# Pooled attention and a GELU mixture layer on one core: the second attention's query casts move into the first MoE, and casts and transposing loads of the first attention are put in another order

## The chip, the core and the metric

The kernel runs on one core of a Trainium2 chip. A core has a matrix engine (TensorE, PE in the profile, with its weight loads as PEld), an engine for elementwise work and reductions (VectorE, DVE), one for functions such as exp and GELU (ScalarE, ACT), a general one (GpSimd, POOL) and SyncE (SP), which here only issues transfers. The engines run their own instruction streams in order and wait for one another through semaphores. Transfers (DMAs) issued by SP and by POOL are carried out by 16 DMA engines; the profile counts the two as queue q1 (SP) and queue q0 (POOL). The metric is device microseconds of one execution. Before the change the median of five runs is 951.9 us (957.32, 951.9, 951.82, 950.97, 953.35).

## The reference

Two stages follow one another: an attention of many queries on pooled keys, and a feed-forward layer with a sigmoid GELU. All inputs and outputs are float32 in memory.

```python
# q (4, 12288, 128), kv (4, 384, 32, 128), w_sr (128, 128)
kv_pool = kv.reshape(B, H // r, r, W // r, r, C).mean(axis=(2, 4))   # r = 4
kv_flat = kv_pool.reshape(B, -1, C) @ w_sr                           # 768 keys
k = v = kv_flat
s = scale * (q @ k.transpose(0, 2, 1))
s = s - s.max(-1, keepdims=True)
a = np.exp(s)
a /= a.sum(-1, keepdims=True) + 1e-09
attn = a @ v
# x = attn as (49152, 128), w_in (128, 2048), w_out (2048, 128)
h = x @ w_in
g = h * (1.0 / (1.0 + np.exp(-1.702 * h)))
out = g @ w_out
```

## The kernel before

**Tiling and stages.** The 49152 queries are cut into 96 groups of 512 (`G`, index i or g) and into 24 supertiles of 2048 (`SG`, index s, four groups each). A batch has 24 groups. The kernel goes through two rounds of 48 groups: first attention (groups 0 to 47), first MoE (the feed-forward layer for the same groups), second attention (48 to 95), second MoE. For one group the attention makes six score tiles, one for each 128 keys; the MoE makes sixteen hidden tiles of 128 features.

**The inner pattern.** `fill_attn` (L337) makes score matmuls into PSUM (L340) for three tiles at a time and ScalarE takes their exponential (L342); `fill_moe` (L583) does the same with L585 and the GELU (L587). `drain_attn` (L344) multiplies the exponentials with the values (L353), and VectorE normalizes the sums into x (L376, L379). `drain_moe` (L589) multiplies with w_out (L595); VectorE transposes the sum back (L606) into one of three buffers, and SP stores it (L608). PE makes fills and drains in turn.

**Who sets the order.** The instruction order of every engine is written out at build time. A loop at the end of the file plans it by a model of costs; `prepare` (L700) calls `background(i)` when the first tile of attention group i is filled, and `background_moe(g)` for an MoE group. These two issue all that the change touches, so "at group i" means this place in the order. The planner's costs do not depend on them.

**Queries.** Queries are needed in bfloat16 and transposed. The first three supertiles are loaded and transposed by PE. For the others `cast_q(s)` (L207, L209) has POOL issue a DMA that reads float32 queries and writes bfloat16 to a scratch tensor `q_bf`, 1 MB read and 512 KB written; later `load_qT(s)` (L212, L215) has SP issue a transposing load from there into one of four buffers qT, after a small memset by VectorE (L214). The load waits for its cast and for the last matmul that read the buffer. `TURN` and `CAST` (L513, L514) say at which group of the first attention each is issued; in the second attention `background` issues load i//4 + 3 and cast i//4 + 5 at every fourth group. Casts 13 to 16 are made in the first MoE at groups 19 to 22.

**Gates.** Before such a DMA `gate` (L506) has VectorE set one element and POOL overwrite it, so that POOL does not issue it before VectorE has come to that place.

**Scores for VectorE.** Some score tiles are not given to ScalarE: for the groups in `rolling` (38, 44, 57, 63, 69, 75, 81, 87) the last of the six, and all six of groups 48 to 51 (`early`), which are made during the first MoE. `early_fill` (L393) has PE compute such a tile (L405) in the midst of other work, and VectorE makes the exponential by a polynomial (L421 on). `early_fits` (L475) lets a rolling tile (i, 5) be made as soon as the groups in work are within one supertile of it: tile 5 of group 38 once group 32 has begun, from query load 9.

**x and its way to the MoE.** x is written by VectorE with queries on partitions, and the MoE needs features there. `put_away(n, m)` (L489, L493) has SP store a part of 24 tiles (six groups) to a scratch tensor `x_bf`, and `bring_back(n, m)` (L496, L499) has SP load it transposed into the same place. In the first attention this is done for parts 0 to 2, at groups 30 to 41, for the rest in the first MoE; in the second attention as the parts are finished. SP's queue is one: query loads, these transfers and output stores are issued in the order of the program.

**Other transfers on POOL.** `load_chunk(1, jc)` at groups 10 and 12 (keys of batch 1), the weights w_in (L540) and w_out (L543), and in the first MoE `add_kv` (L168, L173), eight steps for each of batches 2 and 3, at MoE groups 2 to 9 and 24 to 31.

Of the kernel before, what the change touches and what calls it, by code (L numbers as in the profile page):

```python
# [24 lines left out]
def kernel(  # L25
# [15 lines left out]
    NS = NG // 4  # L41
# [84 lines left out]
    def load_chunk(b, jc):  # L126

        a, ch = divmod(jc, HC)
        t = x_tile(XS - 1 - jc)
        nc.gpsimd.dma_start(out=t, in_=kv_r[b, a, ch])  # L130
        kv_tiles[b, jc] = t.rearrange("p (wp w1 c) -> p w1 wp c", w1=r, c=C)
# [36 lines left out]
    def add_kv(b, n):  # L168
        i, w = divmod(n, r)
        if n == 0:  # L170
            kv_sums[b] = kvsum.tile([Hp, 2, Wp, C], F32, name="kvs")
        for i2 in range(2):
            nc.gpsimd.dma_start(out=kv_sums[b][:, i2], in_=kv_p[b, i, w, :, i2],  # L173
                                **({"accum_op": ADD} if n else {}))
# [32 lines left out]
    def cast_q(s):  # L207
        sl = slice(s * SG, (s + 1) * SG)
        nc.gpsimd.dma_start(out=q_bf[sl, :].rearrange("(p i) c -> p (i c)", p=128),  # L209
                            in_=q_flat[sl, :].rearrange("(p i) c -> p (i c)", p=128))  # L210

    def load_qT(s):  # L212
        qTs[s] = qpool.tile([128, 1, SG], BF, name="qT")
        nc.vector.memset(qTs[s][:, 0, 0:1], 0.0)  # L214
        nc.sync.dma_start_transpose(out=qTs[s], in_=q_bf[s * SG:(s + 1) * SG, :])  # L215
# [273 lines left out]
    def put_away(n, m):  # L489
        size = PART // 2 if n == 0 and m > FIRST else PART  # L490
        for o in range(m * PART, m * PART + PART, size):
            lo = n * XS * SG + o * T
            nc.sync.dma_start(out=x_bf[lo:lo + size * T, :].rearrange("(k p) c -> p k c", p=T),  # L493
                              in_=x[:, o * T:(o + size) * T].rearrange("p (k c) -> p k c", k=size))

    def bring_back(n, m):  # L496
        o = m * PART
        lo = n * XS * SG + o * T
        nc.sync.dma_start_transpose(out=x[:, o * T:(o + PART) * T].unsqueeze(1), in_=x_bf[lo:lo + PART * T, :])  # L499
# [6 lines left out]
    def gate():  # L506

        one = gate_tile[:, gates[0] % 8:gates[0] % 8 + 1]
        gates[0] += 1
        nc.vector.memset(one, 0.0)  # L510
        nc.gpsimd.memset(one, 0.0)  # L511

    TURN = {6: 3, 7: 4, 8: 5, 19: 6, 21: 7, 24: 8, 27: 9, 29: 10, 32: 11, 36: 12}  # L513
    CAST = {0: 5, 13: 6, 14: 7, 19: 8, 22: 9, 25: 10, 28: 11, 32: 12}  # L514

    def background(i):

        first_round = i < GB * 2
        s = TURN.get(i, NS) if first_round else i // 4 + 3 if i % 4 == 0 else NS
        if s < NS:  # L520
            load_qT(s)
        s = CAST.get(i, NS) if first_round else i // 4 + 5 if i % 4 == 0 else NS
        if s < NS:
            gate()
            cast_q(s)
        if i in (10, 12):
            gate()
            for jc in range(i % 10 * 3 // 2, i % 10 * 3 // 2 + 3):
                load_chunk(1, jc)
        if 0 <= i - 16 < JC:  # L530
            extras.append((key_and_value, 1, i - 16))
        if 0 <= i - 15 < JC:
            extras.append((pool_chunk, 1, i - 15))
        if i in (30, 34, 38):
            put_away(0, (i - 30) // 4)
        if i in (33, 37, 41):
            bring_back(0, (i - 33) // 4)
        if i == 26:
            gate()
            nc.gpsimd.dma_start(out=w_in_sb, in_=moe_w_in)  # L540
        if i == 34:
            gate()
            nc.gpsimd.dma_start(out=w_out_sb, in_=moe_w_out.rearrange("(o p) c -> p o c", p=128))  # L543

    def background_moe(g):

        n, g = divmod(g, 4 * XS)
        m, odd = divmod(g - 9, 2)
        m += FIRST
        if n == 0 and FIRST <= m < RT // PART:  # L550
            (bring_back if odd else put_away)(n, m)
        g += n * 4 * XS
        nonlocal low
        if g == 12:
            low = EARLY * JC
            order[:] = [f for f in order if f >= low // K]
        if g == 40:
            background(early[0])
        if 19 <= g < 23:
            gate()  # L560
            cast_q(g - 6)
        if g in (34, 38):
            load_qT(13 + (g - 34) // 4)
        for b, lo in ((2, 2), (3, 24)):
            if lo <= g < lo + 8:
                gate()
                add_kv(b, g - lo)
            if g in (lo + 10, lo + 12):
                use_kv(b, (g - lo - 10) // 2)

    def use_kv(b, a):
        nonlocal extra_at
        sum_kv(b, a)
        on_dve(3.5)
        extra_at = max(extra_at, dve + 1.5)
        extras.extend([(transpose_pooled, b, a), (make_k, b, a), (make_v, b, a)])
# [123 lines left out]
    def prepare(p):  # L700

        nonlocal now
        kind, part = seq[p]
        for i, jc in part:
            if (kind, i) not in begun:
                begun.add((kind, i))
                (background if kind == "a" else background_moe)(i)
            while kind == "a" and ((key_and_value, i // GB, jc) in extras or (transpose_q, i) in extras):
                f, *args = extras.pop(0)
                now = max(now, free[next_acc()]) + COST[f][0]  # L710
                f(*args)
                free[last_acc] = copied(f)
# [73 lines left out]
    for n in range(len(seq)):  # L786
        fill(n + 2)
        jobs(n + 3)
        while True:
# [33 lines left out]
            kind, i, c = source[0]  # L823
# [58 lines left out]
```

## Time and profile before

| what | value |
|---|---|
| median of five runs | 951.9 us (950.97 to 957.32) |
| the profiled execution | 961.65 us |
| its span, first to last instruction | 959.9 us |
| granted TensorE clock, mean | 0.996 |
| ACT busy | 934.3 us |
| PE busy | 936.8 us |
| VectorE busy | 536.6 us |
| SP's queue q1: packets, bytes | 343872, 61.31 MB |
| POOL's queue q0: packets, bytes | 28656, 32.51 MB |
| query casts: number, median time to landing | 21, 6.7 us |
| query loads: number, median time to landing | 21, 7.3 us |
| transposing loads of x: number, median time to landing | 16, 7.6 us |

ACT's timeline gives the stages: the first attention's exponentials run to about 143 us, the first MoE's GELU from 143.8 to about 489, the second attention's from 489 to 615.6, the second MoE's from 616.9 to the end.

How to read it: durations and waits come from one profiled execution; the runs in the first row were made without the profiler. "Time to landing" counts from the issue of a transfer to its last byte's semaphore. A wait in the profile is an idle time of an engine and what ended it. Slices are fortieths of the span, a digit being tenths of busy time.

### The profile page before, as it was taken

Reading aid. Unit: us, or ns where it says so; the run is one execution under the profiler, and the core shown is the slowest. Engines: PE = TensorE matmul, PEld = TensorE weight load, DVE = VectorE, ACT = ScalarE, POOL = GpSimd, SP = SyncE. Lnnn points to the kernel's source line nnn. Section 1 sums busy time; section 2 is a strip of 40 time slices with the busy share of each in tenths; the row PEclk is TensorE's granted clock in tenths of the full one; section 3 lists DMA queues with packets and bytes.
Section 4 is the critical chain, followed back from the end, with each engine's and each line's share of the span. In section 5 each row is a group of like instructions: output and inputs, shape, how many; then the busy total and the mean of one; then the engine's idle time right before and its main releaser. Section 6 shows DMA issues by size and latency. Waiting matters only on the chain.

```text
span 959.9 us, 15315 instructions
## 1 busy us (share of the span) xinstructions
PE 936.8 (98%) x6201; PEld 503.6 (52%) x6314; DVE 536.6 (56%) x1039; ACT 934.3 (97%) x708; POOL 67.4 (7%) x117
## 2 busy tenths in 40 slices
PE   8999999999999999999999969999999999999998
PEld 3677776444444444444447747754444444444444
DVE  4643662111577776877755745365666665556631
ACT  5999999999999999999999959999999999999998
POOL 4100001320000341000000000000000000000000
PEclk9999999999999999999999989999999999999999
DMA  9999983999986898343258995462222222222222
GB/s 182 204 174 161 140 157 53 156 132 159 181 139 92 118 154 102 56 77 55 44 95 160 110 169 119 112 134 41 36 42 39 39 39 39 41 36 43 35 44 45
DMA packets 372871, 94.93 MB, mean 99 GB/s; under 512 B 346736, under 2 KB 370416, under 8 KB 372464
## 3 DMA queue, kind: packets, MB, share of 16 engines
q1 hardware_dynamic: 343872, 61.31, 39.6%
q0 software_dynamic: 28656, 32.51, 22.7%
q8 instruction: 49, 0.80, 0.4%
q14 instruction: 22, 0.18, 0.1%
q10 hardware_dynamic: 272, 0.13, 0.0%
HBM read 52.49 MB, written 48.76 MB: 105 GB/s over the span
## 4 chain that ended last, share of the span: by engine, by line
PE 55%; ACT 40%; DMA 4%; issue 1%; DVE 0%; POOL 0%; POOLq 0%
ACT ag L587 34%; PE banks L595 18%; PE banks L585 17%; PE banks L353 9%; PE banks L340 9%; ACT ag L342 6%; DMA qT<-q_bf 3%; DMA x<-in_kv_dram 1%; PE banks L405 1%; PE banks L139 0%; PE banks L623 0%; PE banks L233 0%; ACT L587 0%; PE banks L161 0%; DVE kT L163 0%
## 5 line engine op out<-in xcount | busy, mean ns | idle before, releaser
L587 ACT ACTIVATE ag<-banks 128x1536 bf16<-128x1536 f32 (+1 forms) x510 | 682.2, 1507 | 0.0
L585 PE MATMUL banks<-x,w_in_sb 128*128 128x512 bf16 x1485 | 407.5, 379 | 2.0 <-ACT ag L587 0.3
L595 PE MATMUL banks<-ag,w_out_sb 128*128 128x512 bf16 x1476 | 403.2, 379 | 1.9
L342 ACT ACTIVATE ag<-banks 128x1536 bf16<-128x1536 f32 (+2 forms) x192 | 246.1, 1424 | 14.0 <-PE banks L340 11.1
L595 PEld LDWEIGHTS <-w_out_sb 128*128 128x128 bf16 x1520 | 148.5, 98 | 178.0 <-issue 0.9
L585 PEld LDWEIGHTS <-w_in_sb 128*128 128x128 bf16 x1522 | 147.3, 98 | 170.4 <-issue 1.1
L606 DVE STREAM_TRANSPOSE o_sb<-banks 128x512 f32<-128x512 f32 x95 | 67.9, 715 | 211.1 <-PE banks L595 197.9
L353 PEld LDWEIGHTS <-ag 128*128 128x128 bf16 x2272 | 146.7, 98 | 47.3 <-issue 2.2
L353 PE MATMUL banks<-v,ag 128*128 128x129 bf16 x2272 | 164.7, 220 | 0.6 <-issue 0.4
L340 PE MATMUL banks<-qT,kT 128*128 128x512 bf16 x499 | 145.8, 380 | 3.5 <-DVE kT L163 1.0
L432 DVE SCALAR_TENSOR_TENSOR ea<-ea,eb 128x512 f32<-128x512 f32 x128 | 87.8, 686 | 3.4 <-issue 0.2
L376 DVE RECIPROCAL rec<-banks 128x3 f32<-128x3 f32 x124 | 22.3, 180 | 97.4 <-PE banks L353 97.2
L379 DVE TENSOR_TENSOR x<-banks,rec 128x384 bf16<-128x384 f32 x124 | 69.1, 557 | 4.3
L340 PEld LDWEIGHTS <-kT 128*128 128x128 bf16 x544 | 46.4, 98 | 26.6 <-DVE kT L163 1.7
L463 DVE RECIPROCAL eb<-ea 128x256 f32<-128x256 f32 x28 | 47.6, 1726 | 0.5
L421 DVE TENSOR_SCALAR ea<-banks 128x512 f32<-128x512 f32 x32 | 22.1, 692 | 41.4 <-PE banks L405 41.1
L173 POOL DMA_DIRECT2D kvs<-in_kv_dram x32 | 40.5, 1308 | 18.1 <-DMA kvs<-in_kv_dram 14.1
L456 DVE SCALAR_TENSOR_TENSOR ea<-ea,eb 128x512 f32<-128x512 f32 x56 | 38.3, 685 | 1.6
L511 POOL MEMSET gate_tile<- 1x1 f32 x39 | 4.1, 106 | 445.4 <-DVE gate_tile L510 445.4
L427 DVE SCALAR_TENSOR_TENSOR eb<-eb,ea 128x512 f32<-128x512 f32 x32 | 22.1, 690 | 0.9
L405 PE MATMUL banks<-qT,kT 128*128 128x512 bf16 x32 | 12.4, 386 | 8.5 <-DMA qT<-q_bf 8.5
L443 DVE TENSOR_SCALAR qT<-banks 128x512 f32<-128x512 f32 x14 | 9.7, 692 | 17.2 <-PE banks L399 16.9
(84 smaller groups left out, 271.1 us busy)
## 6 DMA issues: line engine op xcount, KB each, us to landing
out_dram<-o_sb SPq DMA_DIRECT2D x380, 64.0 KB, 2.0
kvs<-in_kv_dram POOLq DMA_DIRECT2D x32, 384.0 KB, 6.4
q_bf<-in_q_dram POOLq DMA_DIRECT2D x21, 512.0 KB, 6.7
x_bf<-x SPq DMA_DIRECT2D x12, 768.0 KB, 5.8
x<-in_kv_dram POOLq DMA_DIRECT2D x12, 512.0 KB, 10.9
x_bf<-x SPq DMA_DIRECT2D x8, 384.0 KB, 4.0
x<-in_q_dram POOLq DMA_DIRECT2D x5, 256.0 KB, 14.9
w_in_sb<-in_moe_w_in_dram POOLq DMA_DIRECT2D x1, 512.0 KB, 5.4
```

The costliest lines, as they stand in the source:

```text
L173: nc.gpsimd.dma_start(out=kv_sums[b][:, i2], in_=kv_p[b, i, w, :, i2], **({"accum_op": ADD} if n else {}))
L340: nc.tensor.matmul(ps[:, k, :], kTs[i // GB][:, jc * 128:(jc + 1) * 128], rhs, start=True, stop=True)
L342: nc.scalar.activation(place([("a",) + c for c in chunks]), ps, AF.Exp, scale=scale)
L353: nc.tensor.matmul(av_of[u][:, k * (C + 1):(k + 1) * (C + 1)], weights(("a", i, jc))[:, o:o + T], vs[i // GB][:, jc, 0:C + 1], start=(jc = ...
L379: nc.vector.tensor_tensor(to, ps[:, :, 0:C], rec.unsqueeze(2).broadcast_to([128, TS, C]), MUL)
L432: nc.vector.scalar_tensor_tensor(a, a, COEFFS[k], b, ADD, MUL)
L456: nc.vector.scalar_tensor_tensor(a, a, COEFFS[k], b, ADD, MUL)
L463: nc.vector.reciprocal(b[:, m:m + 256], a[:, m:m + 256])
L585: nc.tensor.matmul(ps[:, k, :], w_in_sb[:, fc * 128:(fc + 1) * 128], x[:, g % (4 * XS) * G:(g % (4 * XS) + 1) * G], start=True, stop=True)
L587: nc.scalar.activation(place([("m",) + c for c in chunks]), ps, AF.Gelu_apprx_sigmoid)
L595: nc.tensor.matmul(o_of[g], w_out_sb[:, fc, :], weights(("m", g, fc)), start=(fc == 0), stop=(fc == FCH - 1))
L606: nc.vector.transpose(o_sb, o_of.pop(g))
```

## The change

Casts 17 to 23, made during the second attention before, are made in the first MoE, at groups 33 to 39; casts 13 to 16 move one group later there, to 20 to 23 (`CAST_MOE`). The second attention makes no cast. Query loads 13, 14 and 15 move from MoE groups 34, 38 and 40 to 41, 42 and 43.

In the first attention cast 8 moves from group 19 to 15, casts 9 and 10 are issued together at 25 and casts 11 and 12 at 26. Query loads 6 to 12 are issued at groups 20, 21, 22, 30, 32, 35 and 40 (19, 21, 24, 27, 29, 32 and 36 before). The put-aways of x are issued at 28, 33 and 38 (30, 34, 38), its transposing loads at 31, 36 and 41 (33, 37, 41). The load of w_in moves from 26 to 27 and that of w_out from 34 to 28.

```diff
-    TURN = {6: 3, 7: 4, 8: 5, 19: 6, 21: 7, 24: 8, 27: 9, 29: 10, 32: 11, 36: 12}
-    CAST = {0: 5, 13: 6, 14: 7, 19: 8, 22: 9, 25: 10, 28: 11, 32: 12}
+    TURN = {6: 3, 7: 4, 8: 5, 20: 6, 21: 7, 22: 8, 30: 9, 32: 10, 35: 11, 40: 12}
+    CAST = {0: [5], 13: [6], 14: [7], 15: [8], 25: [9, 10], 26: [11, 12]}
+    CAST_MOE = {20: 13, 21: 14, 22: 15, 23: 16, 33: 17, 34: 18, 35: 19, 36: 20, 37: 21, 38: 22, 39: 23}
...
     def background(i):
...
-        s = CAST.get(i, NS) if first_round else i // 4 + 5 if i % 4 == 0 else NS
-        if s < NS:
+        if i in CAST:
             gate()
-            cast_q(s)
+            for s in CAST[i]:
+                cast_q(s)
...
-        if i in (30, 34, 38):
-            put_away(0, (i - 30) // 4)
-        if i in (33, 37, 41):
-            bring_back(0, (i - 33) // 4)
-        if i == 26:
+        if i in (28, 33, 38):
+            put_away(0, (i - 28) // 5)
+        if i in (31, 36, 41):
+            bring_back(0, (i - 31) // 5)
+        if i == 27:
             gate()
             nc.gpsimd.dma_start(out=w_in_sb, in_=moe_w_in)
-        if i == 34:
+        if i == 28:
             gate()
             nc.gpsimd.dma_start(out=w_out_sb, in_=moe_w_out.rearrange("(o p) c -> p o c", p=128))
...
     def background_moe(g):
...
-        if g == 40:
+        if g in CAST_MOE:
+            gate()
+            cast_q(CAST_MOE[g])
+        if g in (41, 42):
+            load_qT(g - 28)
+        if g == 43:
             background(early[0])
-        if 19 <= g < 23:
-            gate()
-            cast_q(g - 6)
-        if g in (34, 38):
-            load_qT(13 + (g - 34) // 4)
```

## The prediction

> **What bounds the kernel now.** I read the page first: the span, the busy times, the slices.
>
> ```profile
> span 959.9 us, 15315 instructions
> PE 936.8 (98%) x6201; PEld 503.6 (52%) x6314; DVE 536.6 (56%) x1039; ACT 934.3 (97%) x708; POOL 67.4 (7%) x117
> PE   8999999999999999999999969999999999999998
> ACT  5999999999999999999999959999999999999998
> ```
>
> ScalarE (ACT) computes for 934.3 of 959.9 us, and the change gives it no other work: the lists of exponentials and activations, and which of them VectorE makes, stay. The whole prize is ACT's idle time, 25.6 us. The slices put it at the start, at the end, and in one slice near 550 us. The waits and ACT's timeline name that one.
>
> ```profile
> ACT ag L342 <- PE banks L340: 11.1, 5, 9.9
> PE banks L405 <- DMA qT<-q_bf: 8.5, 1, 8.5
> ```
>
> ```profile
> 550.03 4.13 ACT L342 ACTIVATE ag<-banks 128x1536 bf16<-128x1536 f32 x3 [0.26 <-PE banks L340]
> 564.02 1.45 ACT L342 ACTIVATE ag<-banks 128x1536 bf16<-128x1536 f32 x1 [9.85 <-PE banks L340]
> 565.63 1.45 ACT L342 ACTIVATE ag<-banks 128x1536 bf16<-128x1536 f32 x1 [0.16 <-PE banks L340]
> ```
>
> In the second attention TensorE (PE) waited 8.5 us for a transposing load of queries, at a score matmul for VectorE (L405), and ACT behind it lost 9.85 us, 1.4 more than PE (8.47 in PE's timeline). With the two small gaps beside it the stall is 9.85 + 0.26 + 0.16 = 10.3 us. Why the load was late is in the timelines of the SP and POOL queues and in the time that single DMAs took to land.
>
> ```profile
> 528.16 6.61 SPq L499 DMA_TRANSPOSE x<-x_bf  x1
> 534.87 25.44 SPq L215 DMA_TRANSPOSE qT<-q_bf  x2
> ```
>
> ```profile
> 531.13 0.49 POOL L209 DMA_DIRECT2D q_bf<-in_q_dram  x1
> 541.82 0.49 POOL L209 DMA_DIRECT2D q_bf<-in_q_dram  x1
> ```
>
> ```profile
> x<-x_bf SPq DMA_TRANSPOSE x1, 20.3
> q_bf<-in_q_dram POOLq DMA_DIRECT2D x1, 512.0 KB, 19.1
> qT<-q_bf SPq DMA_TRANSPOSE x1, 26.2
> ```
>
> These three are the load of x issued at 528, the cast of 541.8 and the query load of 534.9. Once the casts are over, the same two kinds of load (571.2 and 577.1) take this:
>
> ```profile
> x<-x_bf SPq DMA_TRANSPOSE x1, 8.3
> qT<-q_bf SPq DMA_TRANSPOSE x1, 4.6
> ```
>
> So casts under transposing loads stretch 8.3 to 20.3 and 4.6 to 26.2 us. Now the sum that matters most. The profiled execution took 961.65 us, 1.75 around its span. Without the 10.3 us it would have taken **951.4**. The median of the runs shown is 951.9, the lowest 950.97: the stall is in the profiled execution, and perhaps in the run of 957.32, but hardly in the median one. The change can take 10 us from a profile and about 0.5 from the median.
>
> **The change, part by part.**
>
> *Second attention: seven casts (17 to 23) go.* What remains there is the regime of 567 us on. The load that stalled (issued 534.9, supertile 20 for group 81) would land after 4.6 to 9.1 us (the latter is the row at 519.7, with a cast beside it): 544 at the latest, against PE's stop at 552.65. Gain 10.3 us in the profiled execution; in the median run I take its excess over the floor, 0.5.
>
> *First MoE: those seven casts come to groups 33 to 39, casts 13 to 16 move from 19-22 to 20-23.* Each issues a gate (VectorE memset 59 ns, POOL memset 0.1 us) and one DMA on POOL's queue. The nearest rows are the casts of 279 to 300 us, already in this MoE, landing in 5.9 to 6.7 us while ACT is busy throughout. What hides them: casts have nothing behind them on POOL until the key/value sums begin at group 24 (315.3 us; cast 16, at about 307.5, lands near 314), and the last sum lands at 373.8, before group 33 (380.2). Output stores on SP have three buffers and one group (some 6.75 us) each, so a store a few us late costs nothing. Without that cover one cast would cost its 6 us. Gates: 19 before, 17 after. Zero.
>
> *Query loads 13, 14, 15 move from groups 34, 38, 40 to 41, 42, 43 of the MoE.* ACT's starts of those groups are 436.6, 444.7 and 451.4; the slowest load there took 7.4 us, so they land by 444, 452, 459. They are first read from 487 (13, and 14 by a matmul of L405) and 499 (15, the same way). Their buffers (loads 9, 10, 11) were last read in the first attention. The output stores queued behind them on SP wait for an issue of 1.6 to 5.3 us, inside the buffers' slack. Zero.
>
> *First attention: order on POOL and SP.* Cast 8 goes from group 19 to 15: it then queues behind cast 7 (landed 64.7) at the 2.44 us by which casts 6 and 7 landed one after the other, so it is down at 67.2. Query load 6 (group 20, about 66.3) thus meets almost no cast; at 4.0 to 9.2 us it lands at 70 to 75.5, and PE reads it at about 75.5 (ACT starts that group at 77.5, and PE's timeline fills some 2 us ahead of it). Loads 7 and 8 (69 and 71.6) have over 10 us. The put-aways and returns of x keep landing before the MoE (146.8 us). Weights w_in and w_out come at groups 27 and 28. All zero, but for one edge.
>
> **The edge is query load 9.** It moves from group 27 (issued 85.45) to 30. Its first reader isn't group 36 (ACT 110.0) but a score matmul for VectorE, chunk (38, 5), which the planner places once group 32 has begun:
>
> ```profile
> 100.69 0.38 PE L405 MATMUL banks<-qT,kT 128*128 128x512 bf16 x1
> ```
>
> VectorE's memset for a load stands at 90.96 for group 29 and 99.00 for 32, so load 9 is issued near 93.7 and has 7.0 us. What lies in its way: casts 9 and 10 issued at 79.2, 11 and 12 at 83.2, w_in at 85.3, w_out at 87.2, and on SP put-away 0 at 87.1 (5.7 to 6.4 us). The first cast lands 5.9 us after its issue (row of 79.4), 85.1, the next three at 2.44 each, 92.4; w_in moves as many bytes, 94.9; then w_out, of which no undisturbed row exists (18.9 us amid loads). The rows for a query load, issued at 91.1 (tail of a cast), 85.4 (w_in and a cast), 99.1 (a cast and a put-away):
>
> ```profile
> qT<-q_bf SPq DMA_TRANSPOSE x1, 7.0
> qT<-q_bf SPq DMA_TRANSPOSE x1, 9.5
> qT<-q_bf SPq DMA_TRANSPOSE x1, 12.4
> ```
>
> From 4.6 us (alone) to 12.4, load 9 lands at 98.3 to 106.1, and PE waits 0 to 5.4; with the 1.4 of the known stall ACT loses 0 to 6.8. By the row it is nearest to, 7.0, it lands at 100.7 and nothing is lost.
>
> Here the Trainium skill speaks against the change ("DMA: Bandwidth & Descriptors", section on issuing engines not being separate queues): DMAs from SP and POOL interleave on the same 16 engines, so taking turns in program order frees nothing while the bunch is unfinished. As an estimate by that rule: from 93.7 the engines still owe w_in's last 1.2 us, w_out at no less than 2.44, and the query load's own 4.6, 8.2 in all: landing 101.9, PE waits 1.2, ACT loses up to 2.6, a total of 954.0. By the row it is 951.4. The rows of 20 and 26 us show that sharing can be worse than the rule. I stay with the row, as the unprofiled median shows less of such waits than the profile, and add 0.1 for a rare miss: **951.5**.
>
> **Rivals.**
> 1. *The edge is missed a little* (load 9 takes 8 to 10.4 us): 1 to 4.8 us lost, 952.4 to 956.2; still no measurable change. For: the rule's sum. Against: w_out may be light.
> 2. *Slower: load 9 lands late, at L405 near 100.7.* At 12.4 us the loss is 6.8: **958.2**. It decides from a latency of 10.4 us (0.5% is 4.8 us, less 1.4, gives 3.4 of PE wait). For: w_out took 18.9 us amid loads, and the row of 99.1. Against: no cast is issued after 83.7 until the MoE.
> 3. *Faster:* the stall sits in every run, and an execution without it is quicker than the profile's floor. Time if the median loses 5 us: 946.9. Against: five runs from 950.97 would all have to hold it, beside a floor of 951.4.
> 4. *The change does nothing to the stall*, as the loads slow one another without casts: 951.9. Against: 8.3 and 4.6 from 567 us on.
>
> **How the numbers follow.** 0.5% (4.8 us) is about what a measurement of this kernel can tell from no change: below 947.1, above 956.7. Chances: forecast 0.48, rival 1 0.20, rival 4 0.08, rival 2 0.18, rival 3 0.06. The first three are within, 0.76. The range starts at 949.4, below which only rival 3 and a little luck lie (the stall-free span is 949.6), and ends at 958.2, where rival 2's row ends: about 0.08 is left above and 0.08 below.
>
> **What would show it.** Right: ACT without a gap between 485 and 615; no cast after 425; query loads of 4.6 to 6 and x loads near 8.3 in the second attention; a span near 949.6. At L405 near 100.7 no DMA wait, with load 9 down by then. Wrong: PE waiting there for qT, ACT idle behind it by 1.4 more; or output stores holding VectorE in MoE groups 33 to 43; or a profile without gaps whose runs are yet well under 949, which would mean that the unprofiled runs held stalls unseen.

## The result, and the profile after

Over 44 runs the changed kernel takes 950.99 us in the median (950.48 to 952.62). The kernel before, over 79 runs of the same measurement, takes 953.38 (950.47 to 967.6). The ratio of the means is 0.9962, with a 95% interval of 0.9949 to 0.9975: 0.38% faster (the medians alone differ by 0.25%). Two of the 79 runs, 966.87 and 967.6, over 1.5% above the fastest, are left out of the ratio. The time is inside the range of the prediction and the change, as it said, within 0.5%; but the interval excludes no change, and the gain lies where the prediction had put next to none, in the median run. The five runs shown before had a median of 951.9. The 79 have quartiles of 951.07 and 958.09, a mean of 955.04, and 30 of them are above 956.7. Of the 44 runs after, none is, and the mean is 951.14. So the change hardly moved the best run (950.47 before, 950.48 after). It removed the spread. As the experiments below show, that spread is the stall of the second attention, which cost most executions something, and more than 6 us in 30 of the 79.

The page of the changed kernel, the same rows as before:

```profile
span 949.2 us, 15311 instructions
PE 935.7 (99%) x6201; PEld 503.0 (53%) x6314; DVE 536.8 (57%) x1037; ACT 934.1 (98%) x708; POOL 66.9 (7%) x115
PE   8999999999999999999999999999999999999998
ACT  5999999999999999999999999999999999999998
```

ACT works as long as before (934.1 us against 934.3) and the span of this profiled execution is 10.7 us shorter: all but 0.2 of it is idle time that is gone. The 5 near 550 us is a 9. ACT's timeline across the second attention is now one piece of 86 activations between two table loads:

```profile
487.96 1.28 ACT L342 ACT_TABLE_LOAD   x1
489.26 115.71 ACT L342 ACTIVATE ag<-banks 128x1536 bf16<-128x1536 f32 x86
604.99 1.28 ACT L588 ACT_TABLE_LOAD   x1
```

SP's queue in the stretch of the stall (start, duration, what), and then the time to landing of the load of x at 528 and of the query load at 534:

```profile
528.26 6.03 SPq L499 DMA_TRANSPOSE x<-x_bf  x1
534.39 9.12 SPq L215 DMA_TRANSPOSE qT<-q_bf  x2
```

```profile
x<-x_bf SPq DMA_TRANSPOSE x1, 8.6
qT<-q_bf SPq DMA_TRANSPOSE x1, 5.7
```

They were 20.3 and 26.2 us with casts beside them. The edge that the prediction named is there too. The query load 9 is issued at 93.19, takes this long to land, and PE comes to its first reader at the same moment (PE's timeline; the bracket is the wait):

```profile
qT<-q_bf SPq DMA_TRANSPOSE x1, 7.5
100.78 0.39 PE L405 MATMUL banks<-qT,kT 128*128 128x512 bf16 x1 [0.18 <-DMA qT<-q_bf]
```

### The profile page after: what moved, and what is told of

Same layout as the page of the kernel before. It is cut to its first block, busy times and chain, and to the rows that moved or that the text cites. A ratio compares the mean times of both kernels' runs of the same rounds, so it can differ in the third digit from the quotient of the medians.

```text
span 949.2 us, 15311 instructions
## 1 busy us (share of the span) xinstructions
PE 935.7 (99%) x6201; PEld 503.0 (53%) x6314; DVE 536.8 (57%) x1037; ACT 934.1 (98%) x708; POOL 66.9 (7%) x115
## 4 chain that ended last, share of the span: by engine, by line
ACT 88%; PE 8%; DMA 3%; issue 1%; DVE 0%; POOLq 0%
ACT ag L588 71%; ACT ag L342 16%; PE banks L340 4%; PE banks L353 3%; DMA x<-in_kv_dram 2%; DMA qT<-q_bf 1%; PE banks L586 0%; PE banks L624 0%; PE banks L139 0%; ACT L588 0%; PE banks L596 0%; ACT L342 0%; PE banks L233 0%; PE banks L161 0%; DVE kT L163 0%
## 5 line engine op out<-in xcount | busy, mean ns | idle before, releaser
L340 PE MATMUL banks<-qT,kT 128*128 128x512 bf16 x499 | 145.0, 379 | 3.5 <-DVE kT L163 1.0
L173 POOL DMA_DIRECT2D kvs<-in_kv_dram x32 | 40.4, 1320 | 18.4 <-DMA kvs<-in_kv_dram 15.1
L434 DVE SCALAR_TENSOR_TENSOR ag<-ea,ee 128x512 bf16<-128x512 f32 x24 | 16.5, 688 | 0.7
```

Source lines behind the costliest of these rows:

```text
L340: nc.tensor.matmul(ps[:, k, :], kTs[i // GB][:, jc * 128:(jc + 1) * 128], rhs, start=True, stop=True)
```

## The experiments

Each was timed in turn with the kernel before, on one chip, in four series. "Before" below is its median there, 954.66, 955.06, 954.74 and 953.97 in the four series, with a lowest run of 950.29 to 950.36 each time.

### Which part of the change does it

The seven casts alone, everything else as before:

```diff
-        s = CAST.get(i, NS) if first_round else i // 4 + 5 if i % 4 == 0 else NS
+        s = CAST.get(i, NS) if first_round else NS
...
         if 19 <= g < 23:
             gate()
             cast_q(g - 6)
+        if 33 <= g < 40:
+            gate()
+            cast_q(g - 16)
```

> Before, with casts 17 to 23 alone moved to groups 33 to 39 of the first MoE; the first attention and all query loads stay. Theory (the stall comes from casts in flight beside transposing loads in the second attention): all of the gain, a median of 951.0 to 951.5 and a spread of some 2 us, no DMA wait in the profile's second attention. Rival (the first attention's order is part of the gain): a median above 952, runs up to 957 left.

Measured: 950.58 us (950.40 to 951.74, 14 runs), ratio to before 0.9955 (0.9935 to 0.9976), no DMA wait in its second attention. The casts are all of the gain; it is even 0.4 us under the whole change.

The rest of the change alone:

```diff
-    CAST_MOE = {20: 13, 21: 14, 22: 15, 23: 16, 33: 17, 34: 18, 35: 19, 36: 20, 37: 21, 38: 22, 39: 23}
+    CAST_MOE = {20: 13, 21: 14, 22: 15, 23: 16}
...
+        if not first_round and i % 4 == 0 and i // 4 + 5 < NS:
+            gate()
+            cast_q(i // 4 + 5)
```

> The changed kernel with casts 17 to 23 put back into the second attention, so only the new order of the first attention and the later query loads 13 to 15 are left. Theory: like before, median 952 to 955, runs up to 960 and more, a wait at L405 near 561 us in many executions. Rival (first attention's order pays): at most 952 with a narrow spread.

Measured: 956.19 us (950.76 to 962.61, 14 runs), ratio 1.0005 (0.9975 to 1.0034). The stall is back in its profile at the same place: PE's wait, and the query load behind it.

```profile
PE banks L405 <- DMA qT<-q_bf: 7.5, 1, 7.5
qT<-q_bf SPq DMA_TRANSPOSE x1, 25.6
```

The rest of the change, the new order of the first attention above all, gains nothing by itself that these runs show.

### Which casts

Only casts 22 and 23 back at groups 68 and 72, where x is put away and loaded:

```diff
+    CAST = {..., 25: [9, 10], 26: [11, 12], 68: [22], 72: [23]}
+    CAST_MOE = {..., 36: 20, 37: 21}
```

> The changed kernel with only casts 22 and 23 back in the second attention (groups 68 and 72), where x is put away and loaded transposed. Theory in its narrow form (a cast harms where it meets a transposing load of x): as bad as before, median 952 to 955, runs over 957. Rival (it is the number of casts in that stage): about two sevenths of it, median near 951.6, no run over 954.

Measured: 953.79 us (950.70 to 959.10, 22 runs), ratio 0.9994 (0.9974 to 1.0014); six runs over 956.7. Two of the seven casts bring the slowness back, as the narrow theory has it. Its profiled execution was one of those that escaped (span 949.1 us, no wait at L405 in this stage), but the loads in it are slow all the same, the one of x at 528.1 and the query load at 534.5. The query load landed at 548.9, and PE had stopped for it at 552.65 in the kernel before: a slow load costs nothing until it outlasts that slack.

```profile
x<-x_bf SPq DMA_TRANSPOSE x1, 16.2
qT<-q_bf SPq DMA_TRANSPOSE x1, 14.5
```

The other five back instead, casts 22 and 23 left in the MoE:

```diff
+    CAST = {..., 48: [17], 52: [18], 56: [19], 60: [20], 64: [21]}
+    CAST_MOE = {..., 38: 22, 39: 23}
```

> The changed kernel with casts 17 to 21 back in the second attention (issued at MoE group 43 and at groups 52 to 64), casts 22 and 23 left in the MoE. Narrow theory: no loss, median 951.0 to 951.5, no run over 953; query loads of some 9 us beside a cast, but none over 12. Rival (number of casts): five sevenths of it, median above 952, runs over 955.

Measured: 950.97 us (950.46 to 952.61, 18 runs). Five casts in the second attention cost nothing. The query load issued beside the cast of 509 us landed in 8.8, against 3.7 in the changed kernel without a cast: slower, but far within its slack. So not the number of casts counts, but their place: casts 22 and 23 run beside the loads of x, which begin at 528. What else is particular to that place (a put-away of x stands just before each of these loads) was not varied by itself.

### The edge at query load 9

```diff
-    TURN = {..., 30: 9, 32: 10, 35: 11, 40: 12}
+    TURN = {..., 31: 9, 32: 10, 35: 11, 40: 12}
```

> The changed kernel with query load 9 issued at group 31 in place of 30, some 2.7 us later. Theory (the matmul of L405 near 100.7 us is the first reader, and PE has nothing in hand there): load 9 lands at 102.5 to 103.5, PE waits 1.8 to 2.8 us, ACT loses that and up to 1.4 more, median 952.5 to 955. Rival (the load finds a freer queue when it is later, or PE and ACT make up for it): the same as the changed kernel, within 0.7 us of 951.0.

Measured: 951.15 us (950.58 to 951.99, 22 runs). The load came 1.4 us later, not 2.7 (94.63 against 93.19), and landed at 101.69. In the profile PE waited for it, and ACT lost about the same, not 1.4 more:

```profile
101.74 0.39 PE L405 MATMUL banks<-qT,kT 128*128 128x512 bf16 x1 [1.37 <-DMA qT<-q_bf]
102.98 8.16 ACT L342 ACTIVATE ag<-banks 128x1536 bf16<-128x1536 f32 x6 [1.44 <-PE banks L340]
```

The profiled execution took 951.99 us, the slowest of the 22; the median is that of the changed kernel. So the median is where the rival put it; the matmul of L405 is the first reader and PE does wait, as the theory has it, but too briefly to be seen in the median.

With `27: 9` in its place, so that the load meets the bunch of casts 9 to 12:

> The changed kernel with query load 9 issued at group 27, as before, so beside casts 9 to 12. Theory (in the changed kernel load 9 lands just as it is needed and costs at most 0.3 us): 950.7 to 951.2, that is no difference. Rival (casts under the load stretch it as in the second attention): a landing after 100.7, a wait at L405, 952 or more.

Measured: 952.43 us (951.85 to 954.98, 22 runs), 1.4 above the changed kernel's 950.99; here the rival was right. Issued 8.1 us earlier than in the changed kernel (85.05), the load landed later (102.44), PE waited 2.1 us, and ACT lost 2.14.

```profile
qT<-q_bf SPq DMA_TRANSPOSE x1, 17.4
PE banks L405 <- DMA qT<-q_bf: 2.1, 1, 2.1
```

So letting the casts go first is worth something once they are bunched. What is left of the edge is the end of that bunch, and so w_out was moved behind the query loads:

```diff
-        if i == 28:
+        if i == 41:
             gate()
             nc.gpsimd.dma_start(out=w_out_sb, in_=moe_w_out.rearrange("(o p) c -> p o c", p=128))
```

> The changed kernel with the load of w_out taken from group 28 to group 41, behind the query loads. Theory (what keeps load 9 back in the changed kernel is the end of POOL's bunch, w_out last, and that costs the 0.4 us by which it is above the run that moves the seven casts alone): load 9 lands at 97 to 98.5, no DMA wait at L405, median 950.5 to 950.7. Rival (the 0.4 us lies elsewhere in the first attention or is chance): 951.0 to 951.2, whatever load 9 does.

Measured: 950.50 us (950.30 to 950.69, 12 runs), ratio 0.9958 (0.9932 to 0.9985). Load 9 landed at 98.32, after the time below, and no PE wait for a query load is left.

```profile
qT<-q_bf SPq DMA_TRANSPOSE x1, 5.5
```

The changed kernel itself, put beside three other experiments as a control, gave this:

> The changed kernel itself, beside the others on one chip. 950.9 to 951.2; if it is that, the kernel before with casts of 1 KB (950.56) is 0.4 us faster than it.

Measured: 951.23 us (950.70 to 952.43, 12 runs).

The slowest of the 12 runs with w_out moved (950.69) is not above the fastest of these 12, though they are from another series. By these medians the edge cost the changed kernel 0.5 to 0.7 us, and the version with w_out moved is level with the best found.

### What in a cast does the harm

In the packet records a cast of the kernel before writes one packet of 32 KB on each of the 16 DMA engines; a transposing load consists of 256-byte packets. The cast's two rearrangements were cut into blocks, first in the kernel before:

```diff
-        nc.gpsimd.dma_start(out=q_bf[sl, :].rearrange("(p i) c -> p (i c)", p=128),
-                            in_=q_flat[sl, :].rearrange("(p i) c -> p (i c)", p=128))
+        nc.gpsimd.dma_start(out=q_bf[sl, :].rearrange("(h p i) c -> p h (i c)", p=128, h=4),
+                            in_=q_flat[sl, :].rearrange("(h p i) c -> p h (i c)", p=128, h=4))
```

> Before, with each cast cut into four row blocks, so that a partition's run of it is 2 KB of float32 instead of 8 KB; bytes, places and order stay. Theory of turns by packet (a small packet of a transposing load waits out a long packet of a cast): smaller cast packets shorten the loads, the wait near 561 us is under 4 us or gone, median 951 to 952. Rival (any cast in flight beside a transposing load of x does it, whatever its packets): like before, median 952 to 955, runs over 957.

Measured: 950.56 us (950.30 to 951.04, 20 runs), ratio 0.9945 (0.9928 to 0.9962). No cast was moved, and the stall is gone. First the page's count of POOL's packets in the kernel before, then in this one:

```profile
q0 software_dynamic: 28656, 32.51, 22.7%
```

```profile
q0 software_dynamic: 39072, 32.51, 23.3%
```

The bytes are the same; 10416 packets more over 21 casts are 496 for each, from 16 of 32 KB to 512 of 1 KB. The load of x, the cast and the query load that took 20.3, 17.0 and 26.2 us in the kernel before (issued at 528, 531 and 535) take here, in the same places:

```profile
x<-x_bf SPq DMA_TRANSPOSE x1, 10.8
q_bf<-in_q_dram POOLq DMA_DIRECT2D x1, 512.0 KB, 8.1
qT<-q_bf SPq DMA_TRANSPOSE x1, 8.3
```

The cut shortens the runs that a cast reads as well as those that it writes, so these runs do not tell the two apart.

With 8 KB packets in the kernel before (p=16, h=4 in the same rearrangement):

> Before, with each cast written in runs of 8 KB (four blocks over 16 partitions), between the 32 KB packets of before and the 1 KB of the run that lost the stall. Theory (a load waits out whole packets): between the two, the load of x issued near 528 lands in 11 to 16 us, a median of 950.6 to 952.5, few runs over 955. Rival (any split that makes more than one packet per DMA engine is enough): 950.5 to 950.7, as at 1 KB.

Measured: 951.01 us (950.38 to 955.53, 12 runs; mean 952.23). That lies between, five of 12 runs being over 952. The profiled execution had a stall, PE waiting 2.9 us; its load of x took 18.4 us, outside what was expected, and its query load 20.7.

```profile
x<-x_bf SPq DMA_TRANSPOSE x1, 18.4
qT<-q_bf SPq DMA_TRANSPOSE x1, 20.7
PE banks L405 <- DMA qT<-q_bf: 2.9, 1, 2.9
```

The same 1 KB casts in the changed kernel, and in the one with load 9 at group 27:

> The changed kernel with every cast written in runs of 1 KB (four row blocks), the form that removed the stall from the kernel before. Theory (packets of 32 KB were all that the casts did to the loads, and the changed kernel has nearly none left): 950.4 to 950.8, at most 0.6 us under the changed kernel. Rival (the bunch of four casts ahead of load 9 keeps its cost whatever the packets): 951.0.

> The changed kernel with load 9 at group 27 (17.4 us to landing, a wait of 2.1 us at L405, 952.4 us with whole casts) and with casts in runs of 1 KB. Theory (long packets): load 9 lands in under 12 us, so before 98, no wait at L405, 950.5 to 951.0. Rival (casts queue ahead whatever their packets): 15 us or more, 952 or more.

Measured: 952.22 us (951.41 to 954.36, 12 runs), 1.0 above the changed kernel beside it, and 956.11 (953.07 to 958.11, 12 runs), 3.7 above the same with whole casts. The theory failed in both. The rival failed in the first (951.0) and held in the second, where load 9 took longer yet, 19.5 us:

```profile
qT<-q_bf SPq DMA_TRANSPOSE x1, 19.5
PE banks L405 <- DMA qT<-q_bf: 4.2, 1, 4.2
```

Packets that ended in each 2 us, counted in the records of that execution and of the one with load 9 at group 27 and whole casts:

```
from us                 88   90   92   94   96   98  100  102
1 KB casts   POOL (q0)  346  299  178  204  258  239  295  696
             SP (q1)     98  301  179  201  255  240  297  662
whole casts  POOL (q0)   26   23   95  371  289  665  684  119
             SP (q1)      0   17   95  368  288  667  669 2012
```

Once both queues have packets, they advance one packet for one packet, in both runs. The Trainium skill says this ("DMA: Bandwidth & Descriptors", section on queues, rings and completion order: an engine goes round its queues packet by packet), and these counts agree; it puts several descriptors into a packet, and whether a record here is such a packet no run shows. A query load has 128 packets on each engine and so needs 128 turns. A cast of 1 KB packets offers 32, one of 32 KB offers one, and w_out, 2048 packets of 256 bytes in the records, offers 128 in both runs. With whole casts load 9 therefore takes its turns mostly with w_out, from 94 us on; with 1 KB casts it takes turns with casts from 88 us, and the bunch slows as well: cast 12 landed at 99.17 instead of 93.13, w_in at 101.40 instead of 95.81.

That the turns are the whole of the difference is not shown, and one thing speaks against it. From 96 to 102 us nearly all packets on both queues have 256 bytes in both runs, and yet the load started only 793 of them there with 1 KB casts, against 1624. Of the 793, 163 took more than 200 ns, together 3.6 of the 6 us of an average engine; of the 1624 it was 19, and 1.4 us. Why they are slow stays open. For the first of the two versions, the profiled execution was the fastest of its 12 runs (951.41); it waited 0.9 us at L405 and lost no more elsewhere. Why the median is 1.0 above the control is not settled.

## Why the prediction was right or wrong

**The bound and the prize: right.** ACT's work stayed and the span went to 949.2 us, against a stall-free span of 949.6 worked out before.

**The size of the gain: wrong, in the step "in the median run I take its excess over the floor, 0.5".** The floor was good to 0.4 us against the changed kernel (951.4 against 950.99), and 0.8 too high against the run with the casts alone (950.58). What the median held above it was read from five runs, and the sum went on that the stall is "hardly in the median one". Over 79 runs the median lies 2.4 us and the mean 3.9 above the changed kernel. Rival 3, a stall in every run, was nearer in kind: 49 of the 79 are above 952, against 4 of the 44 after. But some runs have no stall, 5 us in the median was too much, and the floor lay only 0.8 below the profile's, not 4.5. A profile with a 10 us stall and five runs spread over 6.4 us were a sign that executions differ; the middle of five was taken for a state without stall.

**The second attention: right.** The stalled query load landed in 5.7 us where 4.6 to 9.1 was given, by 540 where 544 was the limit. That the casts of this stage are the whole cause was the claim of this part, and the experiment with these casts alone confirms it; that it takes their long packets to do the harm (950.56 us with 1 KB packets in the same places) the prediction did not see. Which two of the seven do it the prediction had before it (the casts of 531.1 and 541.8) but didn't say. Rival 4, loads that slow one another without casts, is excluded.

**The first MoE: right at zero.** No ACT gap appears between 143.86 and the table load at 487.96, and the run with these casts alone is at 950.58.

**The edge: right, in part by luck.** Load 9 was put at 93.7 and landing at 100.7 by the row of 7.0 us; it was 93.19 and 100.73, because an issue 0.5 us early and a load 0.5 us longer (7.5) cancelled. The estimate by the skill's rule gave 101.9, a wait of 1.2 us; the wait was 0.18. The measurement decides for the row, narrowly, though what the estimate counted, the rest of the bunch, is there: with w_out out of the way load 9 landed at 98.32, and the median is 0.5 us lower or more.

Wrong was the addition of 1.4 us to every PE wait. It was taken from a stall of 8.5 us; for waits of 1.37, 2.1 and 2.9 us (load 9 at 31, at 27, and the 8 KB packets) ACT lost 1.44, 2.14 and 2.81. It does hold for the wait of 4.2 us, with 1 KB casts and load 9 at group 27, where ACT lost 5.55 in two gaps:

```profile
105.94 1.45 ACT L342 ACTIVATE ag<-banks 128x1536 bf16<-128x1536 f32 x1 [4.42 <-PE banks L340]
108.52 39.45 ACT L342 ACTIVATE ag<-banks 128x1536 bf16<-128x1536 f32 x29 [1.13 <-PE banks L340]
```

The rows by stretch tell these cases apart by the granted TensorE clock, the third number from the end: behind the stall of 8.5 us, behind the wait of 4.2, and around that of 2.9, each row from its own run:

```profile
560.00:570.00 10.00, 8.83 (x83) 6.36 (x85) 5.34 (x13) 5.83 (x5) 0.00 (x0) 0.78 1.07 225
105.00:110.00 5.00, 4.78 (x36) 3.34 (x35) 3.29 (x7) 2.90 (x2) 0.00 (x0) 0.66 0.69 143
550.00:560.00 10.00, 6.98 (x76) 4.94 (x77) 4.87 (x13) 7.19 (x6) 0.00 (x0) 1.00 1.22 186
```

So the extra loss stands in the executions where the clock had fallen, and rival 2's price of 6.8 us for a wait of 5.4 is not refuted; its landing at 106 did not come.

**Zero for the new order of the first attention: right for time to the nearest us, not to the half.** It cost some 0.5 us, at the edge, and gained nothing: the version without it, and the one with w_out out of the way, are at 950.5 to 950.6.

## What to carry to other kernels

A single profile with a stall, beside five runs spread over 6.4 us as here, calls for many runs before the stall is priced: compare the best runs (950.47 and 950.48 here) to see whether the floor moves, and the spread to see what a stall costs. A transfer that is late may be late because of the shape of another one: casts of one 32 KB packet per DMA engine beside transposing loads cost 10.3 us in the profiled execution, and cutting them into 1 KB rows did as much as moving them. But small packets helped here where a load met one cast, and hurt where it started behind a bunch of transfers; where loads have a deadline, keep bunches away from them.

## What the runs showed that was not expected

In the stall of the kernel before, from 534 to 548 us, SP's queue, that is the transposing loads, has 2172 packets in the records. Of these, 89 took more than 200 ns, many about 2 us, where the median is 18 ns; these 89 hold 10.1 of the 13.1 us that an engine, on the average, spent on that queue. From 534 to 556 us it is this:

| kernel | SP's packets | of them over 200 ns | us in these, of us in all, average engine |
|---|---|---|---|
| before, whole casts | 3962 | 148 | 16.0 of 21.3 |
| before, casts of 1 KB packets | 12981 | 56 | 3.4 of 18.6 |
| changed, no cast there | 14236 | 75 | 5.2 of 21.3 |

The two lower rows include a put-away of x, which is late in the first. So beside whole casts single small packets of the loads hang far more than without, and beside 1 KB casts not more. Why this happens with the loads of x from 528 us on, and hardly where a query load meets a cast of the same form (507 to 519 us: 18 of the 7862 packets of SP's queue, 0.6 us, output stores and a put-away among them), stays open, as does why packets hang in the bunch of the first attention with 1 KB casts. Nor do the runs say what decides in one execution whether there is a stall and how long it is: the order of instructions is the same in all of them.
